# The first batch's scores as plain float32 products, with both heads' keys in one tile

## The chip, the core and the metric

The kernel runs on one core of one Trainium2 chip. The metric is the time of one execution on the device in microseconds (us); the median of the runs counts. The engines are named as in the profile: PE does matmuls (PEld is its weight load), DVE, ACT and POOL do element-wise work, SP issues the DMA transfers.

## The reference

Decay attention over 4 batches, 8 heads, 576 tokens and a head size of 64, followed by two dense layers over the 2304 tokens. Weights come as 64-bit floats, the rest as 32-bit.

```python
scores = scale * np.matmul(q, k.transpose(0, 1, 3, 2))
cum = np.cumsum(np.log(np.clip(f, 0.0001, 1.0)), axis=-1)
decay = cum[:, :, :, None] - cum[:, :, None, :]
scores = np.where(causal, -1000000000.0, scores + decay)
attn = np.exp(scores - max); attn = attn / (sum + 1e-09)
x = (attn @ v)                       # tokens x 512
h = x @ w_in;  g = max(h,0) + alpha * min(h,0);  x = g @ w_out      # 512 -> 2048 -> 512
h = x @ w2_in; g = where(h>=1, h, where(h<=-1, 0, (h+1)**2 / 4));  out = g @ w2_out
```

## The kernel before

All matmul operands that matter for precision are split: a high part rounded to the type float32r (an ACT copy) and a low part that holds the remainder (a DVE subtraction). A product is then two or three float32r matmuls. A plain float32 matmul needs no split.

**Attention.** A unit is a stretch of queries of a batch: tokens 0 to 255, or 256 to 575. Units 0 and 1 are the first batch. For a unit, the heads go in four pairs. For a pair, SP loads K and Q by token (`load_k`, `load_q`); an ACT copy (`dup_q`, line 490) writes the queries twice; PE transposes K (line 512) and Q (line 541, one set for each head) into PSUM tiles of the ring `s`, which has three. Keys of one head: `khi` (ACT, line 523) writes the high part on the head's 64 partitions, `klo` (DVE, line 526) the low part on the other 64, so that one tile `kT` of 128 partitions holds both. `qhi` (line 546) and `qlo` (DVE, line 549) make the two query tiles. The scores of a block of 128 keys are two matmuls (line 615): keys with high queries, keys with low queries. ACT takes them out of PSUM with the decay as a bias (line 628), POOL masks the diagonal block (line 452), the maximum is built on DVE and ACT (lines 647 to 665) and on POOL across partitions (line 671), DVE subtracts (line 687), ACT takes the exponential (line 690), PE multiplies with V (line 724 plain, 730 to 732 split). A block of ones beside V gives the sums; they go through DRAM to be inverted and spread (lines 766 to 795), and the result is written split into the tile `x` (lines 804, 807), which layer 1 reads.

For units 0 and 1 (`plain`) the product with V was plain float32 already (line 724); the scores were split.

**Weights.** Layer 1 has 32 pieces. Each is loaded by SP (line 841) and converted from 64 to 32 bits and split (lines 852 to 890, two passes on ACT and five on DVE). Piece i is loaded only when piece i - `THROTTLE` has been converted. Layer 2's 32 pieces go the same way, once attention has ended and its memory is free.

**Layers.** Tokens go in nine chunks of 256, each in 16 slices of layer 1 (lines 937 to 976: 12 matmuls, two ACT and two DVE passes, 12 matmuls). Chunk 0 needs unit 0, chunk 1 needs unit 1, and slice s needs pieces 2s and 2s + 1. Layer 2 (lines 1112 to 1159) follows.

**Order.** Every operation is a task with an estimated duration and a due position. A planner at build time (`Order.emit`) starts, on each engine, the ready task with the lowest position; its choice is the fixed program order of each engine. Positions of attention in the first batch lie below all others, those of the other batches are spread over the layer 1 slices:

```python
return (x * 24 - 60 if x < 1 else NF + (x - 1) * RATE - LEAD) + off
```

where x is the batch plus the share of it that is done. Buffers come from rings; a task that opens a buffer waits for the users of the one before in its slot. The ring `k` has two slots and a pair took both, one for each head; the ring `q` had two, one for each head's high and low tile.

Of the kernel before, what the change touches and what calls it, by code (L numbers as in the profile page):

```python
# [16 lines left out]
P = 128  # L17
# [174 lines left out]
def kernel(  # L192
# [31 lines left out]
    RATE = 32  # L224
# [5 lines left out]
    THROTTLE = 6  # L230
# [123 lines left out]

    KC = 4 * P
# [28 lines left out]

    RAW = [ap2.tile([P, NKB, 2, D], F32, name=f"raw{i}") for i in range(2)]
# [3 lines left out]
    for t in QR:  # L389
        nc.vector.memset(t[S % P:, 2], 0.0)  # L390
# [65 lines left out]
    for u, pr in head_list():  # L456
# [22 lines left out]
        def load_q(qb_=qb_, b=b, pr=pr, q0=q0, q1=q1):  # L479
            qb_.t = QR[0] if qb_.ring is R["qr"] else ph["qr"]  # L480
            load_tok(qb_.t[:, :, :, 0, :], q, b, pr, q0, q1)
# [10 lines left out]
        T["lq"] = add("ACT", act(-(-n // P) * P), dup_q, p0 - 2, [last["lq"]], use=[qb_])  # L492
# [4 lines left out]
        kx = [Buf(R["k"]) for _ in range(2)]  # L497
        kready = [[], []]

        def k_of(j, kx=kx):  # L500
            if kx[j].t is None:
                kx[j].t = ap1.tile([P, NKB * P], F32R, tag=f"k{kx[j].slot}", name="kT")
            return kx[j].t

        for t0 in range(0, nkp, KC):
# [12 lines left out]
            for j in range(2):  # L518
# [14 lines left out]
        for j in range(2):  # L533
            pb, qb = Buf(R["s"]), Buf(R["q"])
# [9 lines left out]
            def qhi(pb=pb, qb=qb, n=n):  # L544
                qb.t = [ap1.tile([P, NMAX], F32R, tag=f"q{x}{qb.slot}", name=f"q{x}") for x in "HL"]
                nc.scalar.copy(out=qb.t[0][:, :n], in_=pb.t[:, :n])

            def qlo(pb=pb, qb=qb, n=n):
                nc.vector.tensor_tensor(out=qb.t[1][:, :n], in0=pb.t[:, :n], in1=qb.t[0][:, :n].bitcast(F32),
                                        op=ALU.subtract)  # L550
# [3 lines left out]
            h = add("ACT", act(n), qhi, pos_of(2 * pr + j) - 1, [a], new=[qb], use=[pb])  # L554
            qready[j] = [h, add("DVE", dve(n), qlo, pos_of(2 * pr + j) - 1, [h], use=[pb, qb])]
# [36 lines left out]
        for j in range(2):  # L592
# [16 lines left out]
            for x, (kb, qo, m, off) in enumerate(blocks):  # L609
                sb = Buf(R["s"])  # L610

                def qk(sb=sb, kb=kb, qo=qo, m=m, kt=kx[j], qt=qx[j]):
                    sb.t = ps_a.tile([P, 512], F32, tag=f"s{sb.slot}", name="ps_s")
                    for t in range(2):
                        nc.tensor.matmul(out=sb.t[:, :m], lhsT=kt.t[:, kb * P:(kb + 1) * P],  # L615
                                         rhs=qt.t[t][:, qo:qo + m], start=(t == 0), stop=(t == 1))

                a = add("PE", pe(m, 2), qk, pb_, kready[j] + qready[j] + [last_qk], new=[sb], use=[qx[j], kx[j]],
# [611 lines left out]
```

## Time and profile before

| what | value |
|---|---|
| median of 3 runs | 1075.91 us |
| lowest and highest | 1075.69, 1076.36 us |
| profiled execution, its own time | 1075.98 us |
| its span, first to last instruction | 1074.2 us |
| mean granted clock of PE | 0.976 |
| busy share: PE, DVE, ACT, POOL | 95%, 71%, 62%, 13% |

The span is what the trace shows; the profiled execution's time is 1.8 us longer. Busy shares are over the whole span. A granted clock of 1.00 is 2.4 GHz on PE, 0.5 is 1.2 GHz; a value between is a mean over a stretch with both.

### The profile page before, as it was taken

To read this page: it belongs to the slowest core of one execution; us is meant where nothing else is said; L and a number is where in the kernel's file an instruction comes from. 1 tells how busy PE (TensorE), PEld (TensorE's weight loads), DVE (VectorE), ACT (ScalarE), POOL (GpSimd) and SP (SyncE) were. 2 spreads that over 40 slices of the span, in tenths; PEclk is the share of its full clock that TensorE was granted. 3 is DMA by queue.
4 is the path that set the end of the run, shared out by engine and by line. 5 is a ranking of instruction groups with operands and counts; after the bars stand their busy time and mean duration, and the time that the engine had idled before them with its cause. 6 is when DMAs were issued, how large, how long until landed. Compare 5 with 4: busy or idle time off the path is not lost.

```text
span 1074.2 us, 19365 instructions
## 1 busy us (share of the span) xinstructions
PE 1018.5 (95%) x6551; PEld 928.8 (86%) x6551; DVE 766.8 (71%) x1941; ACT 666.0 (62%) x1754; POOL 142.3 (13%) x235
## 2 busy tenths in 40 slices
PE   4678798999999999999999999999999999999998
PEld 3457688999999999999998999988888888888886
DVE  8999997778777787687774999985454445444443
ACT  7878777978888888887773566553343334333332
POOL 3322223222132222322110000000000000000000
PEclk9769988999999999999999999999999999999999
DMA  7664412312124121232103553431011001000001
GB/s 209 155 195 125 121 43 73 78 33 70 25 47 90 34 70 25 51 84 46 50 8 95 175 169 109 151 96 60 1 32 48 0 1 39 1 1 30 10 1 40
DMA packets 125651, 72.28 MB, mean 67 GB/s; under 512 B 89424, under 2 KB 119120, under 8 KB 125552
## 3 DMA queue, kind: packets, MB, share of 16 engines
q1 hardware_dynamic: 125552, 71.04, 24.3%
q8 instruction: 52, 0.85, 0.3%
q14 instruction: 47, 0.39, 0.1%
HBM read 61.42 MB, written 9.51 MB: 66 GB/s over the span
## 4 chain that ended last, share of the span: by engine, by line
PE 77%; DVE 8%; issue 6%; ACT 5%; POOL 2%; DMA 1%; SPq 1%; POOLq 0%; ACTq 0%; DVEq 0%
PE ps_h L1112 18%; PE ps_z L1159 18%; PE ps_y L976 16%; PE ps_h L937 15%; PE ps_s L615 3%; PE ps_o L724 2%; PE ps_o L732 1%; PE ps_o L730 1%; PE ps_o L731 1%; DVE S L687 1%; PE pst L541 1%; PE pst L512 1%; POOL Mb L671 1%; POOL S L452 1%; DVE kT L526 1%
## 5 line engine op out<-in xcount | busy, mean ns | idle before, releaser
L937 PE MATMUL ps_h<-x,w 128*128 128x256 f32 x1728 | 237.2, 287 | 5.9 <-DVE g L950 3.8
L976 PE MATMUL ps_y<-gH,w 128*128 128x256 f32 x1152 | 237.1, 288 | 0.0
L937 PEld LDWEIGHTS ps_h<-x,w 128*128 128x128 f32 x1728 | 219.9, 193 | 8.4 <-DVE g L950 5.2
L976 PEld LDWEIGHTS ps_y<-gH,w 128*128 128x128 f32 x1152 | 190.9, 193 | 0.3 <-ACT gH L956 0.2
L1112 PE MATMUL ps_h<-xw,w 128*128 128x512 f32 x768 | 184.5, 389 | 0.0
L1159 PE MATMUL ps_z<-w,gH 128*128 128x512 f32 x576 | 177.6, 389 | 0.0
L1112 PEld LDWEIGHTS ps_h<-xw,w 128*128 128x128 f32 x768 | 144.1, 188 | 30.0
L976 PE MATMUL ps_y<-gL,w 128*128 128x256 f32 x576 | 164.2, 285 | 1.1 <-DVE gL L959 1.0
L1137 ACT CAST gH<-g 128x256 fp32r<-128x256 f32 x144 | 58.6, 407 | 161.5 <-PE ps_z L1159 160.7
L1140 DVE TENSOR_TENSOR gL<-g,gH 128x256 fp32r<-128x256 f32 x144 | 61.0, 424 | 125.2 <-ACT gH L1137 125.0
L1159 PEld LDWEIGHTS ps_z<-w,gH 128*128 128x128 f32 x576 | 107.3, 188 | 21.4
L1129 ACT ACTIVATE g<-g,half 128x256 f32<-128x256 f32 x144 | 73.3, 509 | 70.0 <-DVE g L1125 69.7
L976 PEld LDWEIGHTS ps_y<-gL,w 128*128 128x128 f32 x576 | 111.1, 193 | 2.0 <-DVE gL L959 1.9
L1159 PE MATMUL ps_z<-w,gL 128*128 128x512 f32 x288 | 112.0, 389 | 0.0
L628 ACT ACTIVATE S<-ps_s,nb 128x320 f32<-128x320 f32 (+3 forms) x224 | 100.2, 449 | 16.9 <-PE ps_s L615 14.8
L452 POOL TENSOR_SCALAR_AFFINE_SELECT S<-S 128x128 f32<-128x128 f32 (+1 forms) x160 | 63.7, 401 | 349.9 <-ACT S L628 340.8
L615 PE MATMUL ps_s<-qH,kT 128*128 128x320 f32 (+3 forms) x224 | 77.2, 345 | 16.1 <-ACT S L628 7.4
L1132 DVE TENSOR_TENSOR g<-ps_h,g 128x256 f32<-128x256 f32 x144 | 61.0, 424 | 39.9 <-ACT g L1129 39.2
L950 DVE SCALAR_TENSOR_TENSOR g<-g,calpha,ps_h 128x256 f32<-128x256 f32 x144 | 68.6, 477 | 27.7 <-ACT g L947 26.6
L671 POOL PARTITION_ALL_REDUCE Mb<-Mx x64 | 78.4, 1225 | 66.9 <-ACT Mx L655 28.0
L690 ACT ACTIVATE S<-S 128x320 f32<-128x320 f32 (+1 forms) x192 | 79.1, 424 | 9.3 <-DVE S L687 8.5
L956 ACT CAST gH<-g 128x256 fp32r<-128x256 f32 x144 | 58.3, 405 | 39.5 <-DVE g L950 32.2
(93 smaller groups left out, 1654.6 us busy)
## 6 DMA issues: line engine op xcount, KB each, us to landing
raw<-in_moe_w_in_dram SPq DMA_DIRECT2D x32, 512.0 KB
raw<-in_moe_w_out_dram SPq DMA_DIRECT2D x32, 512.0 KB
x<-ysb SPq DMA_DIRECT2D x36, 128.0 KB
x<-x SPq DMA_DIRECT2D x9, 512.0 KB
out_dram<-osb SPq DMA_DIRECT2D x18, 256.0 KB
qr<-in_q_dram SPq DMA_DIRECT2D x64, 64.0 KB
raw<-in_k_dram SPq DMA_DIRECT2D x32, 128.0 KB
raw<-in_v_dram SPq DMA_DIRECT2D x24, 128.0 KB
```

Of the source, the lines that this page charges most:

```text
L452: nc.gpsimd.affine_select(out=sl, in_=sl, pattern=[[1, sl.shape[1]]], compare_op=ALU.is_ge, fill=NEG, base=base, channel_multiplier=-1)
L615: nc.tensor.matmul(out=sb.t[:, :m], lhsT=kt.t[:, kb * P:(kb + 1) * P], rhs=qt.t[t][:, qo:qo + m], start=(t == 0), stop=(t == 1))
L628: nc.scalar.activation(out=Sb.t[:, so:so + m], in_=sb.t[:, :m], func=AF.Identity, bias=bias)
L671: nc.gpsimd.partition_all_reduce(Mb.t[:, :n], Mx.t[:, :n], P, ReduceOp.max)
L690: ex = add("ACT", act(gn), lambda Sb=Sb, gn=gn: nc.scalar.activation(out=Sb.t[:, :gn], in_=Sb.t[:, :gn], func=AF.Exp, scale=-SCALE), pb_, ...
L937: nc.tensor.matmul(out=hb.t, lhsT=a[:, sl], rhs=b, start=(cc == 0 and t == 0), stop=(cc == NCC - 1 and t == 2))
L950: nc.vector.scalar_tensor_tensor(out=gb.t, in0=gb.t, scalar=calpha[:, s:s + 1], in1=hb.t, op0=ALU.mult, op1=ALU.add)
L976: nc.tensor.matmul(out=Y[c][e // 2][:, e % 2, :], lhsT=a[:, sl], rhs=b, start=(s == 0 and t == 0 and e % 2 == 0), stop=(s == NF - 1 and t ...
L1112: nc.tensor.matmul(out=hb.t, lhsT=a[:, sl], rhs=b, start=(cc == 0 and t == 0), stop=(cc == NCC - 1 and t == 2))
L1129: nc.scalar.activation(out=gb.t, in_=gb.t, func=AF.Square, scale=0.5, bias=half)
L1132: nc.vector.tensor_tensor(out=gb.t, in0=hb.t[:, hs], in1=gb.t, op=ALU.max)
L1159: nc.tensor.matmul(out=zb[tg].t, lhsT=a[:, sl], rhs=b, start=(s == 0 and t == 0), stop=(s == NF - 1 and t == 2))
```

## The change

For units 0 and 1:

- The queries are loaded without room for a copy, and `dup_q` is left out; the query buffer is read with a denser layout, and its zeroed part is larger.
- One transposed tile holds the keys of both heads, head 0 on partitions 0 to 63 and head 1 on 64 to 127, in plain float32. One ACT copy (`kcopy`) writes it. A pair takes one slot of the ring `k`.
- One set of query transposes serves both heads (`qtr2`). `qcopy` writes each head's queries onto its own 64 partitions of a tile whose other 64 are zero. There are two such tiles for each head; POOL zeroes them once at the start (64x320 each).
- The scores of a block are one plain float32 matmul over 128 partitions; the zeros take the other head's keys out.

For the other units the four query tiles are now two rings of two, one ring for each head, and a head's high and low tile are the two slots of its ring. Two constants change: `RATE` from 32 to 31, `THROTTLE` from 6 to 8.

```diff
@@ -221,13 +221,13 @@
     RC = 3
     LH = 2
     LEAD = 8
-    RATE = 32
+    RATE = 31
     SMALL = 0.28
     GLEAD = 4
     WOFF2 = -5
     WOFF = -8
     AHEAD = 2
-    THROTTLE = 6
+    THROTTLE = 8
     X2T = 768
     SCALE = 1.0 / float(D) ** 0.5
     NC1 = NT // C1
...
@@ -382,12 +383,19 @@
     open_phase(1)
 
 
+    QB = [[ap1.tile([P, NMAX], F32, tag=f"q{j}{x}", name=f"q{j}") for x in range(2)] for j in range(2)]
+    for j in range(2):
+        for t in QB[j]:
+            nc.gpsimd.memset(t[D - j * D:2 * D - j * D], 0.0)
+    R["qp0"], R["qp1"] = Ring(2), Ring(2)
+
+
     RAW = [ap2.tile([P, NKB, 2, D], F32, name=f"raw{i}") for i in range(2)]
     QR = [ap1.tile([P, 3, 2, 2, D], F32, name="qr"), ph["qr"]]
     for t in RAW:
         nc.vector.memset(t[S % P:, NKB - 1], 0.0)
     for t in QR:
-        nc.vector.memset(t[S % P:, 2], 0.0)
+        nc.vector.memset(t[S % P:, 1:], 0.0)
 
     def load_tok(dst, src, b, pr, t0, t1):
         n = (t1 - t0) // P
...
@@ -476,9 +484,11 @@
             kb_.t = RAW[kb_.slot]
             load_tok(kb_.t, k, b, pr, 0, nk)
 
-        def load_q(qb_=qb_, b=b, pr=pr, q0=q0, q1=q1):
+        def load_q(qb_=qb_, b=b, pr=pr, q0=q0, q1=q1, plain=plain):
             qb_.t = QR[0] if qb_.ring is R["qr"] else ph["qr"]
-            load_tok(qb_.t[:, :, :, 0, :], q, b, pr, q0, q1)
+            if plain:
+                qb_.t = qb_.t.rearrange("p c j x d -> p (c j x d)")[:, :3 * P].rearrange("p (c j d) -> p c j d", j=2, d=D)
+            load_tok(qb_.t if plain else qb_.t[:, :, :, 0, :], q, b, pr, q0, q1)
 
         T["lk"] = add("SP", tok_issue(0, nk), load_k, p0 - 3, [last.get("lv"), last.get("lk")], new=[kb_],
                       move=moved(2 * nk, 256))
...
@@ -489,17 +499,17 @@
             t = qb_.t[:, :-(-n // P)]
             nc.scalar.copy(out=t[:, :, :, 1, :], in_=t[:, :, :, 0, :])
 
-        T["lq"] = add("ACT", act(-(-n // P) * P), dup_q, p0 - 2, [last["lq"]], use=[qb_])
+        T["lq"] = last["lq"] if plain else add("ACT", act(-(-n // P) * P), dup_q, p0 - 2, [last["lq"]], use=[qb_])
 
 
         nsplit = sum(y[2] > PVF for y in blocks)
         nkp = -(-nk // P) * P
-        kx = [Buf(R["k"]) for _ in range(2)]
+        kx = [Buf(R["k"]) for _ in range(1 if plain else 2)]
         kready = [[], []]
 
-        def k_of(j, kx=kx):
+        def k_of(j, kx=kx, plain=plain):
             if kx[j].t is None:
-                kx[j].t = ap1.tile([P, NKB * P], F32R, tag=f"k{kx[j].slot}", name="kT")
+                kx[j].t = ap1.tile([P, NKB * P], F32 if plain else F32R, tag=f"k{kx[j].slot}", name="kT")
             return kx[j].t
 
         for t0 in range(0, nkp, KC):
...
@@ -515,7 +525,13 @@
 
             a = last["ktr"] = add("PE", 112 * (t1 - t0) // P, ktr, p0 - 1, [T["lk"], last.get("ktr")],
                                   new=[pb] + (kx if t0 == 0 else []), use=[kb_] + ([] if t0 == 0 else kx))
-            for j in range(2):
+            if plain:
+                def kcopy(pb=pb, t0=t0, t1=t1, k_of=k_of):
+                    nc.scalar.copy(out=k_of(0)[:, t0:t1], in_=pb.t[:, :t1 - t0])
+
+                kready[0].append(add("ACT", act(t1 - t0), kcopy, p0 - 1, [a], use=[pb, kx[0]]))
+                kready[1] = kready[0]
+            for j in range(0 if plain else 2):
                 hr = slice(j * D, (j + 1) * D)
                 lr = slice(D - j * D, 2 * D - j * D)
 
...
@@ -530,8 +546,28 @@
                 kready[j] += [h, add("DVE", dve(t1 - t0), klo, p0 - 1, [h], use=[pb, kx[j]])]
 
         qx, qready = [], [[], []]
-        for j in range(2):
-            pb, qb = Buf(R["s"]), Buf(R["q"])
+        if plain:
+            pb = Buf(R["s"])
+            qx = [[Buf(R[f"qp{j}"])] for j in range(2)]
+            np_ = -(-n // P)
+
+            def qtr2(pb=pb, qb_=qb_, np_=np_):
+                pb.t = ps_a.tile([P, 512], F32, tag=f"s{pb.slot}", name="pst")
+                for c in range(np_):
+                    nc.tensor.transpose(
+                        pb.t[:, c * P:(c + 1) * P], qb_.t[:, c].rearrange("p j d -> p (j d)"), ident)
+
+            a = last["qtr"] = add("PE", 112 * np_, qtr2, p0 - 1, [T["lq"], last.get("qtr")], new=[pb], use=[qb_])
+            for j in range(2):
+                hr = slice(j * D, (j + 1) * D)
+
+                def qcopy(pb=pb, qb=qx[j][0], n=n, j=j, hr=hr):
+                    qb.t = QB[j][qb.slot]
+                    nc.scalar.copy(out=qb.t[hr, :n], in_=pb.t[hr, :n])
+
+                qready[j] = [add("ACT", act(n), qcopy, pos_of(2 * pr + j) - 1, [a], new=qx[j], use=[pb])]
+        for j in range(0 if plain else 2):
+            pb, qb = Buf(R["s"]), [Buf(R[f"qp{j}"]) for _ in range(2)]
             qx.append(qb)
             np_ = -(-n // P)
 
...
@@ -541,18 +577,19 @@
                     nc.tensor.transpose(
                         pb.t[:, c * P:(c + 1) * P], qb_.t[:, c, j].rearrange("p x d -> p (x d)"), ident)
 
-            def qhi(pb=pb, qb=qb, n=n):
-                qb.t = [ap1.tile([P, NMAX], F32R, tag=f"q{x}{qb.slot}", name=f"q{x}") for x in "HL"]
-                nc.scalar.copy(out=qb.t[0][:, :n], in_=pb.t[:, :n])
+            def qhi(pb=pb, qb=qb, n=n, j=j):
+                for b_, x in zip(qb, "HL"):
+                    b_.t = ap1.tile([P, NMAX], F32R, tag=f"q{j}{b_.slot}", name=f"q{x}")
+                nc.scalar.copy(out=qb[0].t[:, :n], in_=pb.t[:, :n])
 
             def qlo(pb=pb, qb=qb, n=n):
-                nc.vector.tensor_tensor(out=qb.t[1][:, :n], in0=pb.t[:, :n], in1=qb.t[0][:, :n].bitcast(F32),
+                nc.vector.tensor_tensor(out=qb[1].t[:, :n], in0=pb.t[:, :n], in1=qb[0].t[:, :n].bitcast(F32),
                                         op=ALU.subtract)
 
             a = add("PE", 112 * np_, qtr, pos_of(2 * pr + j) - 1, [T["lq"], last.get("qtr")], new=[pb], use=[qb_])
             last["qtr"] = a
-            h = add("ACT", act(n), qhi, pos_of(2 * pr + j) - 1, [a], new=[qb], use=[pb])
-            qready[j] = [h, add("DVE", dve(n), qlo, pos_of(2 * pr + j) - 1, [h], use=[pb, qb])]
+            h = add("ACT", act(n), qhi, pos_of(2 * pr + j) - 1, [a], new=qb, use=[pb])
+            qready[j] = [h, add("DVE", dve(n), qlo, pos_of(2 * pr + j) - 1, [h], use=[pb, *qb])]
 
 
         if plain:
...
@@ -609,13 +646,18 @@
             for x, (kb, qo, m, off) in enumerate(blocks):
                 sb = Buf(R["s"])
 
-                def qk(sb=sb, kb=kb, qo=qo, m=m, kt=kx[j], qt=qx[j]):
+                def qk(sb=sb, kb=kb, qo=qo, m=m, kt=kx[0 if plain else j], qt=qx[j], plain=plain):
                     sb.t = ps_a.tile([P, 512], F32, tag=f"s{sb.slot}", name="ps_s")
+                    if plain:
+                        nc.tensor.matmul(out=sb.t[:, :m], lhsT=kt.t[:, kb * P:(kb + 1) * P],
+                                         rhs=qt[0].t[:, qo:qo + m], start=True, stop=True)
+                        return
                     for t in range(2):
                         nc.tensor.matmul(out=sb.t[:, :m], lhsT=kt.t[:, kb * P:(kb + 1) * P],
-                                         rhs=qt.t[t][:, qo:qo + m], start=(t == 0), stop=(t == 1))
-
-                a = add("PE", pe(m, 2), qk, pb_, kready[j] + qready[j] + [last_qk], new=[sb], use=[qx[j], kx[j]],
+                                         rhs=qt[t].t[:, qo:qo + m], start=(t == 0), stop=(t == 1))
+
+                a = add("PE", pe4(m) if plain else pe(m, 2), qk, pb_, kready[j] + qready[j] + [last_qk], new=[sb],
+                        use=[*qx[j], kx[0 if plain else j]],
                         share=min(1.0, m / 256))
                 last_qk = a
                 sbufs.append((sb, a))
```

## Rows read from the trace of the kernel before

**Rows 1.** Engines' busy time in four long stretches, with clock and DMA.
```profile
core 0: us, PE busy (x) PEld busy (x) DVE busy (x) ACT busy (x) POOL busy (x), PEclk, DMA share, GB/s
0.00:180.00 180.00, 132.66 (x720) 112.11 (x721) 166.48 (x403) 137.16 (x338) 51.91 (x79) 0.86 0.49 134
180.00:580.00 400.00, 398.10 (x3231) 394.03 (x3230) 301.97 (x830) 324.96 (x947) 90.41 (x157) 1.00 0.22 50
580.00:715.00 135.00, 132.29 (x1036) 128.63 (x1037) 125.15 (x282) 76.16 (x170) 0.00 (x0) 1.00 0.48 150
715.00:1074.20 359.20, 355.46 (x1569) 294.00 (x1567) 173.16 (x429) 127.70 (x300) 0.00 (x0) 1.00 0.07 23
```

**Rows 2.** The same columns for shorter stretches of the first 180 us.
```profile
40.00:60.00 20.00, 11.16 (x37) 8.53 (x37) 18.28 (x44) 15.57 (x39) 3.37 (x5) 0.59 0.67 192
80.00:100.00 20.00, 18.91 (x140) 17.34 (x140) 19.44 (x48) 15.30 (x38) 4.30 (x6) 1.00 0.50 156
120.00:140.00 20.00, 14.47 (x77) 11.79 (x76) 19.66 (x47) 16.22 (x39) 3.63 (x5) 0.83 0.32 92
160.00:180.00 20.00, 17.59 (x113) 16.29 (x112) 17.33 (x45) 15.29 (x45) 7.66 (x17) 0.84 0.25 63
80.00:180.00 100.00, 84.96 (x548) 75.61 (x548) 94.51 (x229) 76.48 (x191) 27.89 (x41) 0.90 0.33 90
```

**Rows 3.** DVE by shape, 0 to 150 us: count, busy, mean, idle.
```profile
L526 DVE TENSOR_TENSOR kT<-pst,kT 64x512 fp32r<-64x512 f32 x8 | 5.5, 689 | 0.2
...
L549 DVE TENSOR_TENSOR qL<-pst,qH 128x320 fp32r<-128x320 f32 x8 | 3.9, 483 | 0.1
...
L526 DVE TENSOR_TENSOR kT<-pst,kT 64x256 fp32r<-64x256 f32 x8 | 3.4, 422 | 1.5 <-ACT kT L523 1.3
L549 DVE TENSOR_TENSOR qL<-pst,qH 128x256 fp32r<-128x256 f32 x8 | 3.3, 420 | 0.2
...
L526 DVE TENSOR_TENSOR kT<-pst,kT 64x128 fp32r<-64x128 f32 x8 | 2.3, 289 | 0.2
```

**Rows 4.** DVE in order of time: start us, us, what.
```profile
28.71 0.43 DVE L549 TENSOR_TENSOR qL<-pst,qH 128x256 fp32r<-128x256 f32 x1
29.05 0.16 DVE L778 TENSOR_SCALAR rec<-rec 128x4 f32<-128x4 f32 x1
...
173.51 0.70 DVE L890 TENSOR_TENSOR w<-val,w 128x512 fp32r<-128x512 f32 x1
```

**Rows 5.** ACT by line and shape, 0 to 150 us.
```profile
L523 ACT CAST kT<-pst 64x512 fp32r<-64x512 f32 x8 | 4.7, 584 | 0.1
```

**Rows 6.** PE in order of time, two places between 89 and 95 us.
```profile
89.19 0.31 PE L615 MATMUL ps_s<-qH,kT 128*128 128x320 f32 x1
...
89.49 1.60 PE L937 MATMUL ps_h<-x,w 128*128 128x256 f32 x12
...
93.29 0.70 PE L724 MATMUL ps_o<-S,vF 128*128 128x320 f32 x2
...
94.12 0.70 PE L724 MATMUL ps_o<-S,vF 128*128 128x320 f32 x2
```

**Rows 7.** Chain that ended last, 480 to 600 us: start us, us, what.
```profile
485.77 0.45 PE pst L512 x4
...
568.39 1.44 PE ps_y L976 x12
```

**Rows 8.** What PE waited for, 180 to 600 us: us, times, longest.
```profile
PE ps_h L937 <- ACT x L804: 2.1, 1, 2.1
```

**Rows 9.** POOL in order of time, one boundary between two pairs.
```profile
128.32 1.45 POOL L671 PARTITION_ALL_REDUCE Mb<-Mx  x1 [0.51 <-DVE Mx L665]
139.19 0.29 POOL L452 TENSOR_SCALAR_AFFINE_SELECT S<-S 128x128 f32<-128x128 f32 x1 [9.42 <-ACT S L628]
```

**Rows 10.** What SP's queue waited for, 20 to 160 us.
```profile
SPq L396 <- PE ps_o L724: 14.8, 4, 7.0
...
SPq L841 <- DVE w L890: 8.3, 1, 8.3
```

## The prediction, made before the changed kernel was run

> **What bounds the kernel now.** I read the busy time by stretches first, because the share over the span (PE 95%) hides that the program has stages. The four long stretches [rows 1] show it: from 180 us to the end PE is busy nearly all the time at a granted clock of 1.00 (398.10 of 400, 132.29 of 135, 355.46 of 359.20), so there the end moves only if PE work goes away or PE starts sooner. In the first 180 us it is otherwise: PE is busy 132.66 us at a mean clock of 0.86, and DVE 166.48. The short stretches [rows 2] say where: DVE is busy 18.28, 19.44, 19.66 and 17.33 of 20 us, while PE has 1 to 9 us idle in each, and between 40 and 60 us, where it has least to do, its clock is down to 0.59. So in the first stage DVE is the bound. Its queue there holds two kinds of work: the attention of the first batch (units 0 and 1) and the conversion of the 32 pieces of layer 1 weights, which fills each gap. Chunk 0 of layer 1 needs those pieces, two for a slice, and chunk 1 needs unit 1. Both end near 180 us, and from then on PE is full.
>
> So the question for this change is: how much sooner does PE get full, and is PE's own work after that point changed? The diff changes code of units 0 and 1 alone, besides two due-time constants, so PE's instructions after 180 us are the same.
>
> **DVE work that goes.** For the plain units, lines 526 (low part of the keys) and 549 (low part of the queries) are gone. By shape [rows 3]: 3.4 + 5.5 + 2.3 us of line 526 and 3.3 + 3.9 us of line 549, 18.4 us together, 40 instructions, all of units 0 and 1 (4 pairs x 2 heads of each; unit 2 has none of either before 150 us). Neighbours overlap a little: line 549 starts at 28.71 and the next instruction at 29.05, 0.34 us for one listed at 0.43 [rows 4]. I take 0.08 off each of the 16 of line 549: 17.1 us of DVE time. What is added to DVE is the larger zeroing of the two query buffers, at the start. This trace has no such size; bounds are nothing and two passes over 512 columns at 0.69 [rows 3], 1.4 us. I take 0.5, once, ahead of the first keys.
>
> **ACT work that goes.** The doubling of the queries (line 490) goes and the key copy covers 128 partitions at once in place of two copies of 64. On the largest shape the copies take 4.7 us [rows 5], of which half goes. ACT is at 137.16 of 180 [rows 1], so I count all this as nothing for the end; it shortens the chain transpose, copy, scores. Without that slack it would be worth its own time, 2.4 us at least. POOL gets four memsets of 64x320 before its first attention task; at the DVE price above each is under 0.7 us, and POOL is busy 51.91 of 180 [rows 1]: nothing.
>
> **PE work that comes.** A score block was two float32r matmuls and becomes one plain float32 matmul, which the trace records as two instructions, as in line 724. In the hot clock, for 320 columns: the pair takes 0.30 (89.19 to 89.49); a plain block of line 724 followed by one such pair takes 0.83 (93.29 to 94.12) [rows 6], so the plain one takes 0.53, or 1.66 ns a column. That is 0.23 more for a block of 320. For 256, the pair is 2 x 0.12 (1.44 us for twelve [rows 7]) and the plain one 0.425: 0.19 more. For 192, 128 and 64 columns no row gives the pair alone; bounds are 0.24 (as 256) and nothing. With 0.24, the block of 192 costs 0.08 more and the small ones nothing. A head of unit 1 (320, 320, 320, 192, 64) then costs 0.77 more, one of unit 0 (256, 128) 0.19; times eight each, 7.7 us. Query transposes halve (unit 0 from 4 to 2 for a pair, unit 1 from 6 to 3), 20 fewer at 0.11 [rows 7]: -2.2. Net +5.5 us of PE, +10 with the other bound. PE has 47 us idle in this stage [rows 1], so it is costed at nothing now; it is what limits the gain below.
>
> The Trainium skill ("FP8 and Floating Point Precision", TensorE Precision Notes) says that true FP32 takes four passes through the array. By that a block of 320 would go from two passes to four, an estimate of 0.27 us more at one column a cycle; the rows say 0.23. By the page the net would be about 6.7 us in place of 5.5: the rule speaks against the change, and it is the second case below.
>
> **Waits.** The plain units take one key buffer of the ring of two for a pair, where they took both. So the key transposes of the next pair no longer wait for the last scores of this one. Now such a wait shows as a hole in the attention at each pair: POOL's maximum starts at 128.32 and its next mask only at 139.19, 9.42 us idle [rows 9]. The hole is no idle time of DVE, which converts weights in it (19.66 of 20 us [rows 2]), so I give it no price of its own; it lets the attention keep up when the conversions go faster. The later units split four query tiles by head in place of by turn: as many as before, and a head still waits for the scores of the head two before, so nothing. What is late next is the V load, which still waits for the pair before (SP waits 14.8 us on line 724 between 20 and 160 us [rows 10]).
>
> The due times: 8 weight pieces in flight for 6 takes away SP's wait on a conversion (8.3 us, once [rows 10]), behind which the K, Q, V loads and the normaliser's loads queue. RATE 31 for 32 puts the last attention about three layer 1 slices earlier, some 9 us at 2.88 (two groups of twelve [rows 7]). One wait of PE after 180 us is for it: 2.1 us for the x of the last unit [rows 8]. I take 2 us for that; bounds 0 and 2.1. The layer 2 conversions, which keep DVE at 125.15 of 135 [rows 1], start when attention ends; both move together.
>
> **The sum.** From DVE, 17.1 us is the upper bound of the first stage if DVE stays the bound. I don't take all: the first pair's share of it (two of each line, 2 x 0.42 + 2 x 0.34 = 1.5 us [rows 3, 4]) and the 0.5 of zeroing fall where the first loads set the pace, and PE gets near full: between 80 and 180 us it is busy 84.96 of 100 [rows 2] and takes some 4 of the 5.5 us (unit 1's last three pairs), which leaves 11. What was saved before 80 us helps only as far as chunk 0 starts sooner. I take 12. With 2 for the wait: 14 us. The profiled execution took 1075.98 (span 1074.2, 1.8 around it), the median of the runs is 1075.91: 1062 us, or -1.3%.
>
> **Rivals.**
> 1. Forecast: DVE's freed time brings PE's full stage 4 to 18 us sooner, and the wait's 2: 1056 to 1070, chance 0.60.
> 2. PE becomes the bound of the first stage. The added 5.5 to 10 us sit where PE is cold for a part (0.83 to 0.84 from 120 on), and slices of layer 1 queue behind them in order. Then the gain is 11 less what the cold clock adds, some 2 to 7 us with the wait: 1069 to 1073.8. For it: PE 18.91 of 20 at 80 us; against: 14.47 at 120 [rows 2]. 0.13.
> 3. Attention's own chain of loads and masks bounds, not DVE's throughput: the freed DVE time becomes idle time. For it: the holes of 10 us on POOL [rows 9]; against: DVE is busy 19.66 of the 20 us around the one shown [rows 2]. Within 0.2%: 1073.8 to 1078, about 1075. 0.08.
> 4. Slower: the weight loads that may now run two further ahead are in front of K, Q and V in SP's queue and on the DMA engines, which are at 0.67 and 192 GB/s between 40 and 60 us [rows 2]. A piece of 512 KB is 2.7 us at that rate. If each of the 8 pairs waited for two more, that would be 43 us of latency for attention; it decides once more than some 14 us of it is not covered by conversions. I put it at +4: 1080. Against: while fewer pieces were allowed, SP sat waiting for a conversion, so the loads in front are not the scarce thing. 0.10.
> 5. More: with the denser work the clock stays up from 40 to 80 us and from 120 to 180, and the holes close; DVE's 17.1 is then not the limit: 1045 to 1056. 0.09.
>
> **How the numbers follow.** What a measurement of this kernel tells from no change is about 0.2%, 2.15 us. Faster: 0.60 + 0.13 + 0.09 = 0.82; same 0.08; slower 0.10. The range 1052 to 1076 leaves out half of case 5, half of case 3 and case 4, just under 2 in 10.
>
> **What would show it.** Right: lines 526 and 549 absent from units 0 and 1; DVE still at 18 or more of 20 us until the last layer 1 conversion, which starts near 161 us in place of 173.51 [rows 4]; PE full at 1.00 from about 168; the stretch after that as long as now, less 2 us at the last unit. The plain score block at 0.53 hot. Wrong, if DVE has several us idle in each 20 us before 140 (case 3), if PE's busy time is above 19 there while DVE idles (case 2), if SP's issues of K, Q and V come later after each pair (case 4), or if new waits of PE appear between 200 and 580 us, where attention now is denser by a thirtieth, or at the layer 2 conversions.

## The result, and the profile after

The changed kernel takes 1063.26 us (median of 4 runs, 1062.05 to 1065.31), the kernel before 1075.80 on the same chip. The ratio is 0.9887, with a 95% interval of 0.9866 to 0.9908: 1.1% faster. The prediction said 1062.0 with a range of 1052 to 1076. The profiled execution of the changed kernel took 1062.05 us and its span is 1060.3, so 13.9 us of span went, against 14 in the prediction's sum.

The first view to read is again the busy time by stretches (columns as in [rows 1]), long ones and then short ones.

```profile
0.00:180.00 180.00, 146.43 (x813) 119.35 (x814) 162.12 (x393) 139.61 (x360) 56.10 (x89) 0.91 0.52 140
180.00:580.00 400.00, 394.90 (x3209) 391.15 (x3209) 304.43 (x827) 318.07 (x925) 87.06 (x150) 1.00 0.24 56
580.00:715.00 135.00, 134.59 (x1007) 129.02 (x1006) 124.01 (x284) 76.15 (x174) 0.00 (x0) 1.00 0.43 131
715.00:1060.30 345.30, 341.53 (x1507) 282.56 (x1505) 162.70 (x399) 119.63 (x276) 0.00 (x0) 1.00 0.06 20
...
40.00:60.00 20.00, 14.27 (x41) 9.52 (x41) 19.14 (x45) 15.56 (x38) 4.16 (x6) 0.70 0.74 213
60.00:80.00 20.00, 14.14 (x47) 8.96 (x48) 16.81 (x41) 13.13 (x31) 3.98 (x6) 0.74 0.77 221
80.00:100.00 20.00, 18.99 (x126) 16.19 (x125) 19.56 (x48) 16.20 (x40) 6.02 (x7) 1.00 0.46 121
120.00:140.00 20.00, 19.12 (x132) 16.85 (x131) 19.72 (x50) 16.31 (x41) 6.53 (x8) 1.00 0.15 31
160.00:180.00 20.00, 19.65 (x150) 19.36 (x151) 14.39 (x43) 17.38 (x59) 6.62 (x12) 0.91 0.30 76
80.00:180.00 100.00, 94.14 (x648) 84.75 (x648) 93.08 (x233) 80.55 (x218) 30.19 (x46) 0.97 0.31 77
```

Against [rows 1, 2]: in the first 180 us PE is busy 146.43 for 132.66, at a mean clock of 0.91 for 0.86. From 20 to 140 us DVE stays at 19 of 20 us or more but for one stretch, 60 to 80 us, where it is busy 16.81 (19.34 before) and waits 2.8 us for the DMA transfer of the attention's sums. It ran out of work sooner (14.39 for 17.33 between 160 and 180). Between 120 and 140 us PE rose from 14.47 to 19.12 of 20, at 1.00 for 0.83. The second and third row must be read together: between 180 and 580 us PE is busy 394.90 for 398.10, 3.2 us less, and between 580 and 715 us 134.59 for 132.29, 2.3 us more. Most of that is one wait at the place where attention ends, shown below: it came after 580 us before, and comes ahead of it now. Together 0.9 us came back as new idle time.

The next three views are DVE and PE in order of time (start, duration, what), and PE's waits from 180 to 600 us (us, times, longest).

```profile
158.97 0.69 DVE L932 TENSOR_TENSOR w<-val,w 128x512 fp32r<-128x512 f32 x1
```
```profile
91.53 0.71 PE L652 MATMUL ps_s<-q,kT 128*128 128x320 f32 x2
92.08 0.70 PE L766 MATMUL ps_o<-S,vF 128*128 128x320 f32 x2
```
```profile
PE ps_h L979 <- DVE g L992: 2.1, 1, 2.1
PE ps_o L772 <- ACT vH L609: 0.9, 1, 0.9
PE ps_s L656 <- ACT S L670: 0.8, 1, 0.8
```

The last layer 1 conversion starts at 158.97, 14.5 us before that of [rows 4]. A plain score block of 320 columns, hot, goes from 91.53 to 92.08: 0.55 for the 0.53 of the sum. And the wait of [rows 8] for the last unit's x is gone, but PE waits as long, 2.1 us, at the same place for something else, DVE's `g`. DVE in order of time tells why:

```profile
571.89 0.42 DVE L897 TENSOR_SCALAR val<-val 128x512 f32<-128x512 f32 x1
...
574.81 0.69 DVE L914 SCALAR_TENSOR_TENSOR val<-raw,val 128x512 int32<-128x512 int32 x1
575.42 0.87 DVE L992 SCALAR_TENSOR_TENSOR g<-g,calpha,ps_h 128x256 f32<-128x256 f32 x2
```

Attention has ended, so the layer 2 conversions begin, and seven of their passes stand in DVE's order ahead of the `g` of the current slice. (ACT, whose own part of that `g` comes first, reaches it only at 573.37, so not all of the wait is DVE's.)

For the experiments I use a second set of windows, from the start to the moment when the last layer 1 conversion starts. Here is that row of the kernel before, and then of the changed one.

```profile
0.00:173.51 173.51, 126.65 (x695) 106.64 (x695) 161.36 (x388) 131.67 (x319) 47.32 (x68) 0.87 0.49 136
```
```profile
0.00:158.97 158.97, 126.78 (x663) 99.99 (x663) 146.70 (x348) 121.20 (x298) 49.48 (x77) 0.91 0.55 149
```

DVE's busy time falls by 14.66 us, its idle time is 12.15 and 12.27, and the start falls by 14.54. For these two kernels that is the first stage in one line: its length is DVE's work plus 12 us. The end of chunk 0 moved by 10.1 (178.98 to 168.88), that of chunk 1 by 14.8 (253.25 to 238.42).

### The profile page after: what moved, and what is told of

Its sections match the earlier page's. It is cut to its first block, busy times and chain, and to the rows that moved or that the text cites. A ratio compares the mean times of both kernels' runs of the same rounds, so it can differ in the third digit from the quotient of the medians.

```text
span 1060.3 us, 19265 instructions
## 1 busy us (share of the span) xinstructions
PE 1017.5 (96%) x6531; PEld 922.1 (87%) x6531; DVE 753.3 (71%) x1901; ACT 653.5 (62%) x1734; POOL 143.2 (14%) x239
## 4 chain that ended last, share of the span: by engine, by line
PE 81%; DVE 5%; ACT 5%; issue 4%; DMA 3%; SPq 1%; POOL 1%; POOLq 0%; ACTq 0%; DVEq 0%
PE ps_h L1154 19%; PE ps_z L1201 18%; PE ps_y L1018 16%; PE ps_h L979 16%; PE ps_s L656 3%; PE ps_o L766 2%; PE ps_o L772 1%; PE ps_o L774 1%; PE ps_o L773 1%; PE pst L577 1%; DMA sums<-spread 1%; DMA spread<-rec 1%; SPq L404 1%; PE ps_s L652 1%; DMA raw<-in_k_dram 1%
## 5 line engine op out<-in xcount | busy, mean ns | idle before, releaser
L460 POOL TENSOR_SCALAR_AFFINE_SELECT S<-S 128x128 f32<-128x128 f32 (+1 forms) x160 | 61.3, 387 | 336.3 <-ACT S L670 319.7
L729 DVE TENSOR_TENSOR S<-Mb,S 128x320 f32<-128x320 f32 (+3 forms) x224 | 78.7, 397 | 9.7 <-POOL Mb L713 9.1
```

Of the source, the lines that this page charges most:

```text
L460: nc.gpsimd.affine_select(out=sl, in_=sl, pattern=[[1, sl.shape[1]]], compare_op=ALU.is_ge, fill=NEG, base=base, channel_multiplier=-1)
L729: nc.vector.tensor_tensor(out=sl, in0=Mb.t[:, qo:qo + m], in1=sl, op=ALU.subtract)
```

## The experiments

For each kernel the table has the median, and from its profiled execution five marks. The first two are the start of the last layer 1 conversion, and DVE's busy and idle time up to then. Chunk 7 is the chunk that needs the last unit of attention; its end is where DVE first copies its layer 1 result (line 993 before, 1035 after). What comes behind that takes 440.2 to 440.3 us in all of these runs but e7 (441.9), so whatever a run gains or loses, it does so ahead of it. The last two columns split the time up to there: the matmuls that PE has started by 500 us, and PE's idle time and granted clock from 500 us to chunk 7's end, where attention ends. Up to chunk 7's end the changed kernel starts 4354 matmuls, and the runs made from it as many (e4 and e5 9 and 8 more), so their counts can be compared, at some 0.12 us for a hot matmul of 256 columns. Those in brackets cannot: the kernel before and e2 make 20 transposes more, and e7's score blocks are other instructions.

| kernel | us | last conversion | DVE busy + idle | chunk 7 ends | matmuls by 500 us | PE idle, clock from 500 us |
|---|---|---|---|---|---|---|
| before | 1075.8 | 173.51 | 161.36 + 12.15 | 633.93 | (3309) | 2.64, 1.00 |
| changed | 1063.26 | 158.97 | 146.70 + 12.27 | 620.00 | 3388 | 2.16, 1.00 |
| e1 both constants old | 1072.31 | 166.01 | 149.04 + 16.97 | 631.73 | 3336 | 5.31, 0.97 |
| e2 constants alone | 1077.15 | 177.91 | 165.25 + 12.66 | 635.43 | (3294) | 2.17, 0.99 |
| e3 RATE old | 1067.45 | 159.69 | 146.79 + 12.90 | 625.49 | 3388 | 5.29, 0.97 |
| e4 THROTTLE old | 1070.68 | 164.30 | 149.15 + 15.15 | 628.43 | 3341 | 2.03, 1.00 |
| e5 DVE work back, planned | 1099.42 | 177.16 | 165.25 + 11.91 | 657.70 | 3100 | 1.83, 1.00 |
| e6 one key buffer | 1063.19 | 160.34 | 148.60 + 11.74 | 622.01 | 3384 | 2.17, 0.99 |
| e7 one PE pass | 1061.99 | 159.86 | 147.03 + 12.83 | 619.24 | (3338) | 0.49, 1.00 |
| e9 DVE work back | 1086.79 | 183.77 | 171.97 + 11.80 | 644.95 | 3199 | 2.16, 0.99 |
| e10 RATE 30 | 1062.35 | 160.66 | 147.18 + 13.48 | 620.48 | 3373 | 0.99, 1.00 |
| e11 THROTTLE 10 | 1069.05 | 160.44 | 149.33 + 11.11 | 627.46 | 3371 | 4.54, 0.97 |
| e12 less clamping | 1061.07 | 156.43 | 138.67 + 17.76 | 617.26 | 3410 | 2.16, 1.00 |

### The two halves: scores without the constants, constants without the scores

```diff
 e1: the changed kernel        e2: the kernel before
-RATE = 31                     -RATE = 32
+RATE = 32                     +RATE = 31
-THROTTLE = 8                  -THROTTLE = 6
+THROTTLE = 6                  +THROTTLE = 8
```

> The changed kernel with the two old constants (RATE 32, THROTTLE 6). If DVE's freed time is the cause, nearly the whole gain stays: 10 to 13 us faster than before, 1063 to 1066. If the due times are the cause, it falls back to within 4 us of before, 1072 to 1076.

> The kernel before with the two new constants alone. If DVE's freed time is the cause, within 3 us of before (1073 to 1078). If the due times are the cause, 8 us faster or more (1068 or less).

Measured: e1 1072.31 us, ratio to before 0.9969 (0.9959 to 0.9979); e2 1077.15, ratio 1.0016 (1.0004 to 1.0027). So e1 lies where its expectation had it for the due times as the cause, and e2 where its own had it for DVE's freed time: the question of one cause or the other was put wrongly. The new scores alone gain 3.6 us (1075.95 was the kernel before on that chip), the constants alone lose 1.2, and together they gain 12.5. The effects don't add: with the constants in place the scores are worth 13.9 us (1077.15 to 1063.26). The row of e1 to its last conversion and what PE did where attention ends show two places where the rest of the gain went:

```profile
0.00:166.01 166.01, 126.63 (x664) 101.25 (x665) 149.04 (x353) 124.82 (x304) 48.56 (x73) 0.88 0.53 143
```
```profile
574.71 1.24 PE L979 MATMUL ps_h<-x,w 128*128 128x256 f32 x9
581.18 3.62 PE L979 MATMUL ps_h<-x,w 128*128 128x256 f32 x15 [5.23 <-ACT x L846]
```

DVE has lost its work but not all of it as time: it idles 16.97 us, 4.7 more than in the changed kernel, and it does 2.3 us of other work first. And PE, arriving earlier, waits 5.23 us for the last unit's x. A third place, between 300 and 320 us, is shown with e4 below; e1 has it too (140 matmuls there for 156).

### Each constant by itself

```diff
 e3: the changed kernel        e4: the changed kernel
-RATE = 31                     -THROTTLE = 8
+RATE = 32                     +THROTTLE = 6
```

> The changed kernel with RATE at 32 again and THROTTLE left at 8. Theory A: the two constants do two different things. THROTTLE alone lets the first stage use the time that DVE gets free, so chunk 0 still ends near 169 us (last layer 1 conversion near 159), and what RATE gave was only the last unit's x, for which PE then waits 4 to 6 us before chunk 7: 1066 to 1069 us. Rival: RATE also orders the first stage, and without it chunk 0 ends near 173 as with both constants old: 1070 to 1073 us. If RATE is worth nothing beyond the wait of 2.1 us that was priced, 1065.

> The changed kernel with THROTTLE at 6 again and RATE left at 31. Theory A: with six weight pieces allowed in flight the first stage can't use all of DVE's freed time, so chunk 0 ends near 173 us and the last layer 1 conversion near 166 (as with both constants old), while the last unit's x comes in time: 1066 to 1069 us. Rival: THROTTLE is worth nothing, as the prediction had it, and the time stays at 1062 to 1064.

Measured: e3 1067.45 us (0.9927, 0.9912 to 0.9942), e4 1070.68 (0.9958, 0.9944 to 0.9973). Theory A holds for e3: the last conversion starts at 159.69, as in the changed kernel, and by 500 us PE has started the same 3388 matmuls. All of its loss comes after that, where attention ends. PE idles 3.1 us more there, with this row for it, and the lower clock behind the wait (0.97 for 1.00) costs some 2.4 us more of busy time for the same 968 matmuls (120.20 us for 117.84):

```profile
574.81 3.61 PE L979 MATMUL ps_h<-x,w 128*128 128x256 f32 x15 [5.22 <-ACT x L846]
```

For e4 the first stage went as Theory A said (164.30; the chunk 0 end came to 171.4), but the total is 1.7 us above its range, and not for anything where attention ends: from 500 us on PE idles 2.03 us at 1.00, no more than in the changed kernel. By 500 us it is 47 matmuls behind. Most of these were lost between 300 and 320 us, which Theory A didn't have; here is that row of e4, and then of the changed kernel.

```profile
300.00:320.00 20.00, 17.86 (x120) 15.67 (x121) 13.81 (x46) 17.07 (x57) 5.95 (x10) 0.91 0.43 104
```
```profile
300.00:320.00 20.00, 18.98 (x156) 18.23 (x155) 14.92 (x45) 17.00 (x56) 5.81 (x12) 1.00 0.35 87
```

Why attention holds PE up at that place with the old limit was not tested. So RATE 31 is worth 4.2 us, all of it where attention ends, and THROTTLE 8 7.4, all of it ahead of that. The prediction had 2 and nothing.

### DVE's work put back

```diff
 e5: two tasks of the planner for each head, in place of klo and qlo
+add("DVE", dve(t1 - t0), kjunk, p0 - 1, [kready[0][-1]], use=[kx[0]])
+add("DVE", dve(n), qjunk, pos_of(2 * pr + j) - 1, qready[j], use=qx[j])
 e9: inside mx0, unknown to the planner
+if plain:
+    for _ in range(4):
+        nc.vector.tensor_tensor(out=spare[:, :fm // D], in0=seg(Mx.t[:, f0:f0 + fm]),
+                                in1=seg(Mx.t[:, f0:f0 + fm]), op=ALU.subtract)
```

> The changed kernel with DVE's 40 removed instructions put back in number and size, for nobody: they subtract the new key and query tiles from themselves into a part of the x tile that is not used yet, and the scores don't wait for them. If DVE's time alone sets the first stage, 10 to 14 us come back, 1072 to 1077. If it is the shorter chain of keys and queries or the free key buffer, 4 us or less come back, 1063 to 1067.

> The changed kernel with some 17 us of idle DVE work put back into units 0 and 1: behind the first maximum of each head four more DVE operations of its width (128 columns in unit 0, 320 in unit 1) that write to memory nobody reads. The planner doesn't know of them, so the order of every engine is that of the changed kernel; in the earlier run with such work the order changed too. Theory A (DVE's time bounds the first stage): the last layer 1 conversion and the end of chunk 0 move out by 11 to 17 us, to 170 to 176 and 180 to 186, and nothing else changes: 1074 to 1080 us. Rival (the gain is one of order: key buffers, loads and due times, not of DVE's time): less than 5 us, 1063 to 1068.

e5 measured 1099.42 us (1.0221, 1.0203 to 1.0239), far above both of its ranges, so its total doesn't answer the question. Its first stage does: DVE is busy 18.55 us more up to the last conversion, which starts 18.2 us later, and chunk 0 ends 12.0 us later (180.9 for 168.9). But the planner, which knew of the work, made another order of what follows, and between 300 and 350 us PE is busy 40.05 of 50 at a clock of 0.69. e9 keeps every engine's order. It took 1086.79 us (1.0109, 1.0092 to 1.0126), above the 1074 to 1080 that its expectation had for Theory A. The expectation undercounted the work: by shape it is

```profile
L700 DVE TENSOR_TENSOR x<-Mx 128x320 fp32r<-128x320 f32 x32 | 16.1, 504 | 1.1
...
L700 DVE TENSOR_TENSOR x<-Mx 128x128 fp32r<-128x128 f32 x32 | 11.5, 361 | 1.1
```

27.6 us for some 17. Its row up to the last conversion:

```profile
0.00:183.77 183.77, 131.71 (x663) 103.31 (x663) 171.97 (x413) 122.45 (x298) 46.63 (x77) 0.89 0.48 129
```

DVE's busy time grew by 25.3, its idle time fell by 0.5, the last conversion went out by 24.8, and the end by 23.5 (1086.79 less 1063.26). Theory A holds at 0.93 us of time for 1 us of DVE, and the rival (order, not time) falls. As DVE's idle time did not grow, it is DVE's own time that was added, not a wait in the attention's chain, in which these operations stand too.

### PE's added work, and the second key buffer

```diff
 e7: plain units' scores as one float32r product
-F32 if plain else F32R, tag=f"k{kx[j].slot}"
+F32R, tag=f"k{kx[j].slot}"
-QB = [[ap1.tile([P, NMAX], F32, ...
+QB = [[ap1.tile([P, NMAX], F32R, ...
-a = add("PE", pe4(m) if plain else pe(m, 2), qk, ...
+a = add("PE", pe(m, 1 if plain else 2), qk, ...
 e6: a pair takes both key slots
-kx = [Buf(R["k"]) for _ in range(1 if plain else 2)]
+kx = [Buf(R["k"]) for _ in range(2)]
-use=[*qx[j], kx[0 if plain else j]],
+use=[*qx[j], *(kx if plain else [kx[j]])],
```

> The changed kernel with the plain units' scores as one float32r product (keys and queries only rounded, so the scores are less exact): the 0.53 us block becomes about 0.15, 9 to 12 us less PE work in the first stage and nothing else changed. If PE's added work is covered, within 2 us of the changed kernel, 1061 to 1065. If PE bounds the first stage too, 3 to 9 us faster than it, 1054 to 1060.

> The changed kernel, but a pair of units 0 and 1 takes both slots of the key ring, as it did before, so that the next pair's key transposes wait for this pair's last scores. DVE's work is that of the changed kernel. If DVE's time alone made the gain, as the prediction had it (no price for the second key buffer): 1062 to 1065 us, chunk 0 end within 2 us of 169. Rival: the second buffer is what lets attention fill the time that DVE gets free; then the holes on POOL come back at 9 to 10 us for a pair, and the first stage gets 4 to 10 us longer: 1066 to 1072.

e7 took 1061.99 us (0.9873, 0.9856 to 0.9890), e6 1063.19 (0.9883, 0.9864 to 0.9902). In e7 PE is busy 12 us less up to its last conversion (114.69 for 126.78), and the time moves by 1.3: PE's added work is covered, and rival 2 falls. (The planner knew of the lower cost, so the order is not quite the same.) In e6 the time doesn't move by anything that can be measured: the second key buffer has no price, as predicted, though one hole on POOL is 15.48 us long where the longest in the changed kernel is 10.54.

```profile
0.00:159.86 159.86, 114.69 (x601) 95.89 (x602) 147.03 (x350) 123.07 (x300) 49.90 (x75) 0.94 0.54 148
```
```profile
148.27 0.60 POOL L460 TENSOR_SCALAR_AFFINE_SELECT S<-S 128x128 f32<-128x128 f32 x1 [15.48 <-ACT S L670]
```

### Further along the same way

```diff
 e10                 e11                    e12, in clamp()
-RATE = 31          -THROTTLE = 8           +c = slice(0, 1 if layer == 1 else DM)
+RATE = 30          +THROTTLE = 10          -out=vb.t, in0=vb.t, ...
                                            +out=vb.t[:, c], in0=vb.t[:, c], ...
 e8, plain units' blocks of 64 to 192 columns
+eng = nc.gpsimd if plain and m < 256 else nc.vector
-nc.vector.tensor_tensor(out=sl, in0=Mb.t[:, qo:qo + m], in1=sl, op=ALU.subtract)
+eng.tensor_tensor(out=sl, in0=Mb.t[:, qo:qo + m], in1=sl, op=ALU.subtract)
...
```

> The changed kernel with RATE at 30. If the step from 32 to 31 paid by bringing the last unit's x ahead of PE's need (PE's wait of 5.2 us for it went), there is nothing left of it to gain, and only the wait of 2.1 us for DVE's g at the start of the layer 2 conversions may move: 1061 to 1064 us, same as the changed kernel. Rival (denser attention lets layer 1 end sooner still): 1056 to 1060. Third: the attention now crowds DVE between 180 and 550 us, so that PE waits there: 1065 to 1070.

> The changed kernel with THROTTLE at 10. From 6 to 8 was worth 7.4 us in the changed kernel: DVE's idle time up to the last layer 1 conversion fell from 15.2 to 12.3 us. If loads in flight are still the limit, DVE's idle time falls further and the time is 1057 to 1061 us. Rival: the 12 us that are left are gaps between instructions and the start, as in the kernel before (12.2 us too), and more loads in flight only stand ahead of K, Q and V in SP's queue: 1062 to 1068.

> The changed kernel with DVE work taken away in the other half of its first stage: the clamp of each layer 1 piece (32 instructions, 15.0 us of DVE in the profile of the changed kernel) is done for one column of 512 only, so the kernel leaves out the clamping of nearly all magnitudes. The planner counts it as whole, so the order of every engine is that of the changed kernel. Theory A (DVE's time still bounds the first stage after the change, at 1 us for 1 us): the last layer 1 conversion starts at 144 to 147 us and the time is 1048 to 1052 us. Rival 1 (the change has brought the bound to PE, which then is full): the conversions end sooner but the time is 1056 to 1062. Rival 2 (the weight loads bound the conversions): DVE's idle time up to the last conversion grows from 12.3 us by more than 7, and the time is 1056 to 1062 too; DVE's idle time and PE's busy time tell the two apart.

> The changed kernel with more work taken from DVE: in units 0 and 1 the subtraction ahead of the exponential goes to POOL for the blocks of 64, 128 and 192 columns (32 instructions, some 7.5 us of DVE's first stage in the profile of the changed kernel), while the blocks of 256 and 320 stay on DVE. The planner knows of it. Theory A (each microsecond of DVE work in the first stage is a microsecond of the end, and DVE's idle time there stays at 12 us): the last layer 1 conversion starts near 152 us and the time is 1055 to 1058 us. Rival 1 (POOL is slower at it and lies in the attention's chain, maximum across partitions included, so attention comes later): DVE's idle time grows by what it lost in work, 1062 to 1068. Rival 2 (PE is now the bound of the first stage): PE busy near 19.5 of 20 from 80 us on, gain under 3 us, 1060 to 1063.

e10: 1062.35 us (0.9879, 0.9864 to 0.9894), the same as the changed kernel, as expected; PE's idle time where attention ends is down to 0.99, and by 500 us it is 15 matmuls behind. e11: 1069.05 (0.9940, 0.9928 to 0.9953), slower than with 8 and above both of its ranges, and not for the reason its rival gave: the first stage is that of the changed kernel (last conversion at 160.44, idle 11.11). By 500 us it is 17 matmuls behind, and the larger part of the loss is where attention ends, in PE's idle time (4.54 for 2.16) and its clock behind the wait (0.97):

```profile
578.18 2.93 PE L979 MATMUL ps_h<-x,w 128*128 128x256 f32 x12 [3.91 <-DVE g L992]
```

e12: 1061.07 (0.9873, 0.9857 to 0.9890), 2.2 us under the changed kernel by the medians, with intervals that overlap. The clamp's 32 instructions still take 4.6 us for one column each, so 10.4 us went, not 15. DVE is busy 8.0 us less up to the last conversion, but idles 5.5 more (short of the 7 that rival 2 asked for), and PE is full for a stretch. Here are two rows of e12, and then the changed kernel's for the second stretch:

```profile
0.00:156.43 156.43, 122.63 (x663) 97.49 (x663) 138.67 (x349) 120.85 (x298) 46.47 (x77) 0.90 0.55 152
80.00:140.00 60.00, 59.55 (x397) 52.38 (x396) 57.05 (x146) 50.10 (x125) 16.69 (x22) 0.99 0.31 77
```
```profile
80.00:140.00 60.00, 58.11 (x388) 50.54 (x387) 59.22 (x145) 49.15 (x121) 18.59 (x23) 1.00 0.31 78
```

PE at 59.55 of 60 between 80 and 140 us is what rival 1 of that run names. But 3.0 of the 5.5 us that DVE idles more lie ahead of 80 us, where PE is busy 48.73 of 80, so that PE is what takes over is not shown. Either way, DVE work that is still taken out is worth a fifth of a microsecond for one or less, where DVE work put in costs 0.93: the change ends close to the point at which DVE is no longer the bound. Whether a newly planned order would use more of it was not tried. e8 went wrong altogether, 1245.04 us; see the last section.

## Why the prediction was right, and where its terms were not

**DVE is the bound of the first stage: shown.** The sum took 17.1 us of DVE time as the most and 12 as the likely gain, with the last conversion near 161. It started at 158.97, and DVE's busy time up to it fell by 14.66. The difference to 17.1 has a row: the conversions' passes of 512 columns got slower on the mean (line 914, 760 ns a pass for 701 before; line 932, 731 for 695), which is 2.9 us over 30 pieces; the last section says which passes these are. The zeroing cost 0.4 more, as taken. At the end of chunk 1 all of the 14.5 us are still there, more than the 12 that the sum took.

```profile
L914 DVE SCALAR_TENSOR_TENSOR raw<-raw,val 128x512 int32<-128x512 int32 x30 | 22.8, 760 | 0.3
L932 DVE TENSOR_TENSOR w<-raw,w 128x512 fp32r<-128x512 f32 x30 | 21.8, 731 | 0.4 <-ACT w L927 0.2
```

**PE's added work is covered: shown** by e7. The block price was right (0.55 for 0.53). (The prediction's second figure for PE's net, 6.7 us, takes its price for the blocks of 320 and 256 columns alone; with the smaller blocks priced alike it is 8.5, and the 12 us of e7 cover that as well.)

**The due times: the step that was mis-sized.** "I take 2 us" for RATE, and nothing for THROTTLE, priced the constants by the waits of the kernel before. Undone one by one in the changed kernel they are worth 4.2 and 7.4 us, undone together 9.0. What the runs show is that the waits moved with the change. In the kernel before, DVE was full while SP waited for a conversion (8.3 us [rows 10]), and raising the limit of six along with RATE gained nothing there (e2). With less work on DVE the old limit leaves DVE idle (15.15 us in e4 for 12.27) and 2.4 us of other work stands ahead of the last piece; SP's wait for a conversion is there in e4, 6.9 us in two. That it is this wait that costs the time is argued, not shown: in the changed kernel SP waits at the same line 5.9 and 3.6 us for other work of DVE, and the larger part of e4's loss lies between 300 and 320 us, for a reason that is open. For RATE it is shown: the last unit's x, 2.1 us late before, is 5.2 us late once PE comes sooner. The sum came out because what it gave wholly to DVE (12) holds only with both constants in place: with the old ones 3.6 us are left.

**The wait at the last unit** was to go, worth 2 us. It went, and a wait of the same length for `g` took its place: from 500 us to chunk 7's end PE idles 2.16 us for 2.64, so 0.5 us were gained. The prediction named new waits "at the layer 2 conversions" among what would make it wrong; this is one, of 2.1 us.

**So the total of 14 came out partly by luck.** Up to chunk 7's end 13.9 us went: PE's idle time fell from 51.5 to 38.7 us and its busy time by 1.1. By stretches, PE's idle time fell by 14.2 us in the first 200 us, grew by 1.8 between 200 and 500, in new waits that the sum did not have, and fell by 0.5 after that. The first stage gave more than the 12, and that made up for the wait that stayed and the ones that came.

**The other rivals.** PE as the bound (2): one of its two signs is there, PE above 19 of 20 us from 100 to 140, but not the other, as DVE is full too (59.22 of 60 from 80 to 140). Attention's own chain (3): DVE's idle time up to the last conversion did not grow (12.27 for 12.15), so no. Loads ahead of K, Q and V (4): the constants alone did lengthen the first stage of the kernel before, by 4.4 us (177.91 for 173.51), of which 1.2 were left at the end; that the loads did it was not shown, as DVE's busy time grew by 3.9 us and its idle time by 0.5. In the changed kernel the last conversion came 14.5 us sooner all the same. More than predicted (5): the clock did rise (0.70 for 0.59 between 40 and 60 us, 1.00 for 0.83 between 120 and 140), but the last conversion came sooner by as much as DVE's work fell, and by no more.

## What to carry to other kernels

Where one engine is full for a whole stage, add up its busy and idle time to the stage's last instruction: a change of its work shows there at close to one for one, until something else is the bound, and one run that takes away still more tells how near that is. Before a loss is put down to a place, take a mark behind which all runs need the same time, and count the work done ahead of it: a mark at the end of one chunk moves with the program's order. Limits and due times that cost nothing now must be priced again at the state after the change: a limit hidden behind a full engine can become a wait once that engine has less to do, and a value that was a little late is later by what its reader gained. When part of a joint change is tested, run both halves, since neither half alone may gain anything.

## What the runs showed of the hardware

**POOL pays for changing between two kinds of instruction.** e8 moved 24 short subtractions to POOL (its expectation says 32; the trace has 8 each of 64, 128 and 192 columns) and lost 182 us. Its POOL in order of time and by line, with the idle time before each:

```profile
106.22 0.45 POOL L730 TENSOR_TENSOR S<-Mb,S 128x128 f32<-128x128 f32 x1 [6.92 <-issue]
106.63 0.54 POOL L460 TENSOR_SCALAR_AFFINE_SELECT S<-S 128x128 f32<-128x128 f32 x2
113.15 1.08 POOL L713 PARTITION_ALL_REDUCE Mb<-Mx  x1 [5.98 <-issue]
121.00 0.45 POOL L730 TENSOR_TENSOR S<-Mb,S 128x128 f32<-128x128 f32 x1 [6.76 <-issue]
```
```profile
L713 POOL PARTITION_ALL_REDUCE Mb<-Mx x15 | 17.6, 1175 | 94.3 <-issue 93.8 <-ACT Mx L697 0.5
...
L730 POOL TENSOR_TENSOR S<-Mb,S 128x128 f32<-128x128 f32 x8 | 3.6, 445 | 64.1 <-issue 64.1
```

Each maximum across partitions that follows a subtraction, and each subtraction that follows a maximum, stands behind 6 to 8 us in which POOL waits for nothing that the trace shows: in the first 300 us 93.8 us for 15 of the one, 6.3 each, and 64.1 for 8 of the other, 8.0 each. The instructions themselves are short (0.45 and 1.08). In the changed kernel the masks of line 460 alternate with the same maximum, and no such gap is there. The Trainium skill ("GPSIMD Engine Reference", 2.1 Instruction dispatch) states that the first call to a freshly loaded kernel of this engine pays about 6 us with no visible instruction. The size agrees with the trace, but here the gap is there at every turn from one to the other, not once; that it is the same cost is not shown.

**DVE passes that start beside POOL's maximum are longer.** In the changed kernel 14 passes of 512 columns took 0.87 to 1.21 us up to the last conversion, where the others take 0.39 to 0.78. Each of them starts within 0.65 us of the start of a maximum across partitions (line 713) on POOL. One such pair, POOL and DVE, with the next pass:

```profile
71.15 1.61 POOL L713 PARTITION_ALL_REDUCE Mb<-Mx  x1 [0.60 <-DVE Mx L707]
```
```profile
71.57 1.21 DVE L914 SCALAR_TENSOR_TENSOR raw<-raw,val 128x512 int32<-128x512 int32 x1
72.81 0.70 DVE L919 SCALAR_TENSOR_TENSOR raw<-raw 128x512 int32<-128x512 int32 x1
```

The kernel before has 7 such passes, each beside a maximum too. The middle value of line 914 is the same in both kernels (0.686 and 0.685 us), so its slower mean comes from more of these meetings, not from slower passes throughout. That the maximum is the cause is not tested by a run.

**PE's clock after a wait.** After the idle time of 5.23 us in e1, fifteen matmuls of layer 1 took 3.62 us where twelve take 1.60 hot, and the granted clock was 0.73 between 580 and 590 us. After 3.91 us in e11 twelve took 2.93. After 2.06 us it went either way, in the same place and with the same 401 matmuls from chunk 6's end to chunk 7's. Here is that stretch of the changed kernel, and then of e6:

```profile
569.89:620.00 50.11, 48.05 (x401) 47.85 (x400) 45.32 (x101) 23.78 (x58) 0.00 (x0) 1.00 0.52 159
```
```profile
570.40:622.01 51.61, 49.55 (x401) 49.35 (x400) 45.39 (x101) 24.88 (x58) 0.00 (x0) 0.97 0.52 154
```

In the changed kernel and e12 the twelve behind the wait took 1.70 and the clock stayed at 1.00; in e2, e6 and e9 they took 1.99 to 2.58, and the stretch was 1.5 us longer. So a late value can cost more than its wait: e3's costs some 2.4 us on top, and one as short as 2.06 us nothing or 1.5.
